# First bias tiles loaded from GpSimd's queue, and the second pair's q, k loaded earlier and cast by VectorE

## The chip, the cores and the metric

The kernel runs on one core of a Trainium2 chip. The metric is the time of one execution on the device in microseconds (us), as the median of several runs. A core has five engines with instruction queues of their own: TensorE (matmuls and transposes; PE in the profile, PEld its weight loads), VectorE (DVE), ScalarE (ACT), GpSimd (POOL) and SyncE (SP), which here only issues transfers. All transfers run on the core's 16 DMA engines. A queue works in order: an instruction that waits holds up all that stands behind it on its engine.

## What is computed

The reference is attention with a learned bias on relative positions, followed by a feed-forward layer with the mish function:

```python
# q, k, v: (4, 8, 576, 64); w_in: (512, 2048); w_out: (2048, 512); all float32
scores = scale * np.matmul(q, k.transpose(0, 1, 3, 2))
rel = (pos[:, None] - pos[None, :]).astype(np.float32)
psi_rel = np.log1p(np.abs(rel))
psi_i = np.log1p(np.maximum(pos[:, None].astype(np.float32), 1.0))
x = (psi_rel / psi_i)[..., None]
h = np.maximum(x @ w1 + b1, 0.0)
bias = h @ w2                                   # (576, 576, 8)
scores = scores + bias.transpose(2, 0, 1)[None, :, :, :]
scores = scores - np.max(scores, axis=-1, keepdims=True)
attn = np.exp(scores)
attn = attn / (np.sum(attn, axis=-1, keepdims=True) + 1e-09)
attn_out = np.matmul(attn, v)
...
h = x @ w_in                                    # x: the 2304 tokens of attn_out
g = h * np.tanh(np.log1p(np.exp(np.minimum(h, 20.0))))
out = g @ w_out
```

## The kernel before

The kernel has three phases: the bias for all heads, the attention, and the feed-forward layer. The change touches the first phase and its seam with the second.

**The bias phase** (loop at line 551, 36 tiles of 16 query rows). For each tile `make_h` (line 510) writes four tiles ht on VectorE or ScalarE, `mirrored` (line 524) multiplies them by w2 on TensorE into PSUM, and `evac` (line 534) copies the result out as bt, on ScalarE nearly always (line 538; once on VectorE, line 540), and has SyncE store it to DRAM, in the buffer bias_d (line 545). Eight buffers bt are in use. The rows of one bias tile of the attention come from 8 such tiles (4 for the tile number 4); the order of the five tiles is ORDER = 0, 1, 4, 2, 3.

**The bias loads.** `load_bias` (line 194) brings one tile of the first head pair back from DRAM, in three pieces of 288, 256 and 32 KB for 128 rows (lines 200 to 202), or in two pieces of 144 KB for tile number 4 (line 205). All are issued by SyncE, at the iterations BIAS_AT = 12, 20, 24, 30 and 37. Each waits for the stores that wrote its rows, and SyncE's other transfers stand behind it.

**q and k.** A pair is one batch and two heads; there are 16. For the matmuls in float32r each pair's q, k (128x1280) are split in a rounded part qkhi and a rest qklo. `load_hi` (line 182) has GpSimd load q, k with a cast to float32r, `load_raw` (line 170) has SyncE load them as they are in rawqk, and `split_qk` (line 188) has VectorE subtract one from the other. Three buffers qkhi and two buffers rawqk are in use. GpSimd's queue holds nothing else in the first phases, so that its loads for the pairs 0, 1 and 2 all start at the beginning, and the next when a buffer comes free. For pair 1, `load_raw` and `load_v` (line 176) stand at iteration 36 of the loop (lines 570 to 572), behind the last store; the last bias tile is loaded at iteration 37, and behind it `load_weights` (line 94) loads two weight tiles of 512 KB.

**The attention** goes in steps, five for each pair, one for each block of query rows in ORDER. A step has `scores` on TensorE (line 224, three products of the split parts), `add_bias` on VectorE, which adds the bias out of the tile and keeps the extreme value of each row (line 238, for 128 rows two halves of 576 columns, each reading its own part of the bias tile), `exps` on ScalarE (line 253), then, two steps later, `transposes` (lines 293 to 320), whose results ScalarE or VectorE copies out of PSUM (line 307 and others), and `pv_duo`, the products with v (lines 335, 339), at whose end VectorE copies the result x (line 342). There are two PSUM buffers s for scores; a step with 128 rows needs both, so its scores wait for the bias addition of the step before. Steps 0, 1 and 2 are spread over the bias phase (SOFT_AT = 18, 27, 35); step 3 and on run in `step` (line 413). `ahead` (line 379) loads what later pairs need, and `split` (line 400) calls `split_qk(i + 1)` at the third step of a pair, for the first pair at step 3. Step 4 (`late`) has its parts in another order than all others: transposes of step 2, products with v, and only then its scores and bias addition. Step 5 is the first of pair 1 and needs qkhi and qklo of pair 1; step 7 splits pair 2, and step 10 needs it.

Of the kernel before, what the change touches and what calls it, by code (L numbers as in the profile page):

```python
# [8 lines left out]
F32R = mybir.dt.float32r  # L9
# [6 lines left out]
B, H, S, D, C = 4, 8, 576, 64, 32  # L16
# [3 lines left out]
P = 128  # L20
SH = S // 2
QW = 1280
# [6 lines left out]
ORDER = [0, 1, 4, 2, 3]  # L29
# [15 lines left out]
def kernel(ctx: ExitStack, tc, qk, v, wb, w2, w_in, w_out, psia, psi4, rinv, eye, out):  # L45
    nc = tc.nc
    pe, dve, act, pool, sp = nc.tensor, nc.vector, nc.scalar, nc.gpsimd, nc.sync
# [115 lines left out]
    hip = rsbuf("hip", 2, side="right")  # L163
# [3 lines left out]
    qk_raw, qk_hi, qk_lo, v_t, bias_t = {}, {}, {}, {}, {}  # L167
    st.tile([P, 32], F32, name="fill", bufs=1)

    def load_raw(i):  # L170
        hp, b = divmod(i, B)
        raw = rawp.tile([P, QW], F32, name="rawqk")
        sp.dma_start(out=raw, in_=qk[b, hp])
        qk_raw[i] = raw

    def load_v(i):
        hp, b = divmod(i, B)
        vt = vp.tile([P, 2, 5, D], F32, name="vt")
        sp.dma_start(out=vt, in_=v[b, hp].rearrange("p (h c d) -> p h c d", h=2, c=5))
        v_t[i] = vt  # L180

    def load_hi(i):
        hp, b = divmod(i, B)
        hi = hip.tile([P, QW], F32R, name="qkhi", bufs=3)
        pool.dma_start(out=hi, in_=qk[b, hp])
        qk_hi[i] = hi

    def split_qk(i):

        lo = hip.tile([P, QW], F32R, name="qklo")  # L190
        dve.tensor_tensor(lo, qk_raw.pop(i), qk_hi[i].bitcast(F32), op=ALU.subtract)
        qk_lo[i] = lo

    def load_bias(hp, c):
        h0, h1 = 2 * hp, 2 * hp + 1
        rows = P if c < 4 else 64
        src = bias_d[c][:, :rows * PITCH].rearrange("h (i j) -> h i j", j=PITCH)[:, :, PAD:PAD + S]
        t = bias_t[hp, c] = biasp.tile([P, 2 * S if c < 4 else 640], F32, name=f"bias{c}")[:, :2 * S if c < 4 else S]
        if c < 4:
            sp.dma_start(out=t[:, 0:S], in_=src[h0])  # L200
            sp.dma_start(out=t[:, S + 64:], in_=src[h1, :, 0:512])
            sp.dma_start(out=t[:, S:S + 64], in_=src[h1, :, 512:S])
        else:
            for r in range(2):
                sp.dma_start(out=t[r * 64:r * 64 + 64], in_=src[h0 + r])

    NPAIR = B * HP
    steps = [(i, c) for i in range(NPAIR) for c in ORDER]
# [46 lines left out]
    def reciprocals(i):  # L255

        r = sums.pop(i)
        dve.tensor_scalar(r, r, 1e-9, None, op0=ALU.add)
        dve.reciprocal(r, r)
        return r  # L260
# [151 lines left out]

    def step(n):
        i, x = divmod(n, 5)
        late = n == 4

        def begin():
            if n < NS:
                scores(n)
                add_bias(n)  # L420

        def end():
            if n < NS:
                exps(n, 0)
                exps(n, 1)
                ahead(n)
            if 0 <= n - 1 < NS and (n - 1) % 5 == 4:
                rc[n - 1] = reciprocals((n - 1) // 5)
            if n < NS:
                split(n)  # L430
            if turned:
                store_reciprocals()


        if not late:
            begin()
        for k in {3: (0, 1)}.get(n, (n - LAG,)):
            if 0 <= k < NS:
                transposes(k)
        if not late:  # L440
            end()

        if late:
            for k in range(5):
                pv_duo(0, 0, k)
        for j, grp, ks in {4: ((i, 0, (0, 1)),), 0: ((i - 1, 0, (2, 3)),), 1: ((i - 1, 0, (4,)),),
                           2: ((i - 1, 1, (0, 1, 2)),), 3: ((i - 1, 1, (3, 4)),)}[x]:
            if 0 <= j < NPAIR and (j, grp) != (0, 0):
                for k in ks:
                    pv_duo(j, grp, k)  # L450
        if late:
            begin()
            end()

# [20 lines left out]
    NB = len(ts)  # L477
    NW = S + 15

    def reach(t):  # L480

        left, right = 16 * t + 15, S - 16 * t
        n = max(left + 1, right)
        return left, right, n + n % 2
# [5 lines left out]
    BIAS_AT = (12, 20, 24, 30, 37)  # L490
# [6 lines left out]
    for idx in range(NB + 2):  # L497
# [4 lines left out]
        if idx + 2 < NB:  # L502
            n = reach(ts[idx + 2])[2]
# [47 lines left out]
    for idx in range(NB + 2):  # L551
        if idx < NB:
            make_h(idx + 2)
            mirrored(idx)
        if 1 <= idx <= NB:
            evac(idx - 1)
        if idx == 1:
            load_raw(0)
            load_v(0)
        if idx == 12:  # L560
            split_qk(0)
        if idx in BIAS_AT:
            load_bias(0, ORDER[BIAS_AT.index(idx)])
        for lag, do in enumerate((scores, add_bias, exps)):
            if idx - lag in SOFT_AT:
                for u in range(2 if lag == 2 else 1):
                    do(SOFT_AT.index(idx - lag), *((u,) if lag == 2 else ()))
        if idx == 33:
            load_hi(1)
        if idx == NB:  # L570
            load_raw(1)
            load_v(1)
        if idx == NB + 1:
            load_weights()
    bias_scope.close()

# [10 lines left out]
    for n in range(len(SOFT_AT), NS):  # L587
        step(n)
# [246 lines left out]
```

## Time and profile before

| | us |
|---|---|
| median of 3 runs | 699.02 |
| lowest and highest | 698.3, 699.84 |
| the profiled execution | 701.45 |
| its span, first to last instruction | 699.5 |

| engine | busy, share of the span |
|---|---|
| TensorE matmuls | 97% |
| VectorE | 74% |
| ScalarE | 66% |
| GpSimd | 2% |

The bias phase fills the first 55 us or so of the span, the attention goes on to about 270 us, and the rest is the feed-forward layer. Times in the profile are counted from the first instruction. Busy shares are means over phases with different limits; what a change in one place is worth is read from that place, from the waits there.

### The profile page before, as it was taken

The numbers are of one execution on the slowest core, as the hardware profiler recorded it, in microseconds if no ns is written. First come the engines' busy times: TensorE is split into PE (matmuls) and PEld (weight loads), VectorE is DVE, ScalarE is ACT, GpSimd is POOL, SyncE is SP. The second block draws the span as 40 slices with busy tenths as digits, with TensorE's granted clock in tenths as the row PEclk, the third lists the DMA queues.
The fourth block names the chain that finished last, engine by engine and source line by source line (L and its number), as shares of the span: only waits on it lengthen the run. The fifth ranks groups of instructions, "written<-read, shape, count | busy, mean of one in ns | idle before, by whom it ended". The sixth has DMA issues, their size and how long they took to land.

```text
span 699.5 us, 14139 instructions
## 1 busy us (share of the span) xinstructions
PE 675.6 (97%) x5456; PEld 515.5 (74%) x5456; DVE 514.3 (74%) x1051; ACT 463.9 (66%) x980; POOL 16.5 (2%) x26
## 2 busy tenths in 40 slices
PE   6987999999999999899999999999999999999997
PEld 3545766666666676567878888889988888888886
DVE  7894788888888886468888888776776567665554
ACT  6994899999989999645665556554544455444443
POOL 1000000000000002000000000001000000000000
PEclk9999899999999999999999999999999999999999
DMA  7989658659657762412231221323040000010001
GB/s 257 294 263 303 221 178 290 211 172 314 228 180 250 252 208 76 130 48 61 60 121 60 91 66 55 121 73 109 1 121 31 0 1 0 1 61 0 1 0 61
DMA packets 46435, 86.94 MB, mean 124 GB/s; under 512 B 13200, under 2 KB 22048, under 8 KB 46368
## 3 DMA queue, kind: packets, MB, share of 16 engines
q1 hardware_dynamic: 43488, 75.32, 33.5%
q0 software_dynamic: 2304, 10.49, 4.7%
q8 instruction: 43, 0.70, 0.4%
q10 hardware_dynamic: 576, 0.22, 0.1%
q14 instruction: 24, 0.20, 0.1%
HBM read 64.56 MB, written 21.45 MB: 123 GB/s over the span
## 4 chain that ended last, share of the span: by engine, by line
PE 85%; DVE 7%; ACT 3%; DMA 3%; issue 1%; SPq 0%; DVEq 0%; ACTq 0%
PE y L679 25%; PE h L634 24%; PE s L224 11%; PE o L335 10%; PE tp L293 5%; PE bps L532 5%; PE o L339 2%; PE tp L309 2%; DMA rawqk<-in_qk_dram 1%; DMA xlo<-r_d 1%; DVE e L657 1%; DVE e L641 1%; DVE e L656 1%; ACT bt L538 1%; DVE w L127 1%
## 5 line engine op out<-in xcount | busy, mean ns | idle before, releaser
L238 DVE CUSTOM_DVE_ANT_0 pt<-s,bias 128x576 f32<-128x576 f32 x144 | 103.7, 754 | 44.4 <-PE s L224 44.3
L253 ACT ACTIVATE pt<-pt,m 128x576 f32<-128x576 f32 x144 | 112.5, 792 | 6.5 <-DVE m L238 6.2
L658 ACT CAST ghi<-e 128x512 fp32r<-128x512 f32 x72 | 44.7, 621 | 105.5 <-DVE e L657 98.2
L679 PE MATMUL y<-who,ghi 128*128 128x512 f32 x288 | 112.5, 391 | 2.2 <-ACT ghi L658 1.4
L679 PE MATMUL y<-who,glo 128*128 128x512 f32 x288 | 112.4, 390 | 1.1 <-DVE glo L661 1.0
L679 PE MATMUL y<-wlo,ghi 128*128 128x512 f32 x288 | 112.2, 390 | 0.0
L634 PE MATMUL h<-xhi,whi 128*128 128x512 f32 (+1 forms) x320 | 80.0, 370 | 1.3 <-ACT xhi L609 1.3
L661 DVE TENSOR_TENSOR glo<-e,ghi 128x512 fp32r<-128x512 f32 x72 | 49.7, 691 | 42.0 <-ACT ghi L658 41.3
L307 ACT COPY main<-tp 128x512 f32<-128x512 f32 x126 | 68.1, 597 | 18.4 <-PE tp L293 18.0
L634 PE MATMUL h<-xhi,wli 128*128 128x512 f32 (+1 forms) x320 | 79.6, 371 | 0.0
L634 PE MATMUL h<-xlo,whi 128*128 128x512 f32 (+1 forms) x320 | 79.2, 369 | 0.0
L335 PE MATMUL o<-main,vt 128*64 128x320 f32 (+1 forms) x512 | 75.8, 418 | 1.1 <-DVE x L342 1.1
L639 ACT ACTIVATE e<-h 128x512 f32<-128x512 f32 x72 | 42.6, 592 | 45.7 <-PE h L634 45.7
L640 DVE TENSOR_SCALAR e<-e 128x512 f32<-128x512 f32 x72 | 30.7, 426 | 55.8 <-ACT e L639 55.8
L634 PEld LDWEIGHTS h<-xhi,whi 128*128 128x128 f32 x320 | 57.4, 189 | 13.6 <-ACT xhi L609 2.7
L634 PEld LDWEIGHTS h<-xhi,wli 128*128 128x128 f32 x320 | 57.5, 190 | 10.1
L634 PEld LDWEIGHTS h<-xlo,whi 128*128 128x128 f32 x320 | 57.4, 190 | 10.2
L679 PEld LDWEIGHTS y<-who,ghi 128*128 128x128 f32 x288 | 54.1, 188 | 14.4 <-ACT ghi L658 2.2
L679 PEld LDWEIGHTS y<-who,glo 128*128 128x128 f32 x288 | 54.1, 188 | 13.5 <-DVE glo L661 2.3
L679 PEld LDWEIGHTS y<-wlo,ghi 128*128 128x128 f32 x288 | 54.1, 188 | 10.8
L657 DVE TENSOR_TENSOR e<-e,r 128x512 f32<-128x512 f32 x72 | 49.9, 693 | 7.5
L224 PEld LDWEIGHTS s<-qkhi 64*128 64x128 f32 (+1 forms) x288 | 25.0, 189 | 36.9 <-DVE m L238 16.2
(71 smaller groups left out, 1037.6 us busy)
## 6 DMA issues: line engine op xcount, KB each, us to landing
bias_d<-bt SPq DMA_DIRECT2D x36, 295.5 KB
qkhi<-in_qk_dram POOLq DMA_DIRECT2D x16, 640.0 KB, 6.4
rawqk<-in_qk_dram SPq DMA_DIRECT2D x16, 640.0 KB
w<-in_w_in_dram SPq DMA_DIRECT2D x16, 512.0 KB
w<-in_w_out_dram SPq DMA_DIRECT2D x16, 512.0 KB
vt<-in_v_dram SPq DMA_DIRECT2D x16, 320.0 KB
bias<-bias_d SPq DMA_DIRECT2D x16, 288.0 KB
out_dram<-w SPq DMA_DIRECT2D x17, 256.0 KB
```

What stands on the lines that cost most here:

```text
L224: pe.matmul(live[n][h][:, j, :SH], stat[rows, c * P:(c + 1) * P], mov[rows, k0:k0 + SH], start=(k == 0), stop=(k == 2))
L238: dve.tensor_tensor_reduce(out=halves(pt[:, sl]), in0=s[:, :, :SH], in1=halves(bt[:, sl]), scale=-0.125, scalar=BIG, op0=ALU.add, op1=ALU. ...
L253: act.activation(ps, ps, AF.Exp, bias=m[:, u:u + 1], scale=-1.0, accum_out=sums[i][:, k:k + 1])
L293: pe.transpose(tp[:, k * 64:(k + 1) * 64], pt[rows, c0:c0 + P], ident[rows, rows])
L307: (dve.tensor_copy if n < 2 and u else act.copy)(blocks[:, :, off + 64 * u:off + 64 * u + 64], tp)
L335: pe.matmul(o[h * 64:h * 64 + 64, :w], vt[:, h, k, :], main[:, h, k, :], start=(k == 0), stop=False, **kw)
L634: pe.matmul(h[:, u * n:(u + 1) * n], w["i", g4, d][:, r * P:(r + 1) * P], x[:, d, :n], start=(k == 0), stop=(k == 11))
L639: act.activation(e, h, AF.Exp)
L657: dve.tensor_tensor(e, e, r, op=ALU.mult)
L658: act.copy(ghi, e)
L661: dve.tensor_tensor(glo, e, ghi.bitcast(F32), op=ALU.subtract)
L679: pe.matmul(ys[blk][t], g[:, c0:c0 + P], w, start=((blk, f) in first and k == 0), stop=((blk, f) in last and k == 2))
```

## The change

`load_bias` gets a parameter with the queues of its pieces. In the bias phase the tiles 0, 1, 4 and 2 are issued wholly by GpSimd, and the last, tile 3, by SyncE but for its 256 KB piece, which GpSimd issues. (The calls from `ahead` for the later head pairs stay on SyncE.) `load_hi(1)` at iteration 33 is gone: `split_qk` for pair 1 makes qkhi on VectorE as a copy of rawqk with the cast to float32r, and then subtracts as before. `load_raw(1)` moves from iteration 36 to 26. `load_v(1)` moves from iteration 36 to 37, behind the last bias load, and `load_weights` follows it. Step 4 loses its order of its own: its scores and bias addition come first, then the transposes of step 2, the exponentials, and the products with v last.

```diff
     def split_qk(i):
 
+        if i == 1:
+            qk_hi[i] = hip.tile([P, QW], F32R, name="qkhi", bufs=3)
+            dve.tensor_copy(qk_hi[i], qk_raw[i])
         lo = hip.tile([P, QW], F32R, name="qklo")
...
-    def load_bias(hp, c):
+    def load_bias(hp, c, queues=(sp, sp, sp)):
...
         if c < 4:
-            sp.dma_start(out=t[:, 0:S], in_=src[h0])
-            sp.dma_start(out=t[:, S + 64:], in_=src[h1, :, 0:512])
-            sp.dma_start(out=t[:, S:S + 64], in_=src[h1, :, 512:S])
+            queues[0].dma_start(out=t[:, 0:S], in_=src[h0])
+            queues[1].dma_start(out=t[:, S + 64:], in_=src[h1, :, 0:512])
+            queues[2].dma_start(out=t[:, S:S + 64], in_=src[h1, :, 512:S])
         else:
             for r in range(2):
-                sp.dma_start(out=t[r * 64:r * 64 + 64], in_=src[h0 + r])
+                queues[r].dma_start(out=t[r * 64:r * 64 + 64], in_=src[h0 + r])
...
     def step(n):
         i, x = divmod(n, 5)
-        late = n == 4
...
-        if not late:
-            begin()
+        begin()
         for k in {3: (0, 1)}.get(n, (n - LAG,)):
             if 0 <= k < NS:
                 transposes(k)
-        if not late:
-            end()
-
-        if late:
+        end()
+
+        if n == 4:
             for k in range(5):
                 pv_duo(0, 0, k)
...
-        if late:
-            begin()
-            end()
...
         if idx in BIAS_AT:
-            load_bias(0, ORDER[BIAS_AT.index(idx)])
+            load_bias(0, ORDER[BIAS_AT.index(idx)], (sp, pool, sp) if idx > NB else (pool, pool, pool))
...
-        if idx == 33:
-            load_hi(1)
-        if idx == NB:
+        if idx == 26:
             load_raw(1)
+        if idx == NB + 1:
             load_v(1)
-        if idx == NB + 1:
             load_weights()
```

## Rows read from the trace of the kernel before

**Rows 1.** The page: span, TensorE's busy time, its granted clock in 40 slices.

```profile
span 699.5 us, 14139 instructions
PE 675.6 (97%) x5456; PEld 515.5 (74%) x5456; DVE 514.3 (74%) x1051; ACT 463.9 (66%) x980; POOL 16.5 (2%) x26
...
PEclk9999899999999999999999999999999999999999
```

**Rows 2.** Chain of waits from 54 us on: start, us, what.

```profile
57.26 7.68 DMA rawqk<-in_qk_dram
...
68.26 1.68 PE s L224 x11
...
83.91 1.00 PE s L224 x12
...
98.31 0.99 PE s L224 x12
```

**Rows 3.** Timeline of VectorE, 58 to 68: start, us, engine, line, operation [idle before].

```profile
58.50 1.49 DVE L307 COPY main<-tp 128x512 f32<-128x512 f32 x2
65.03 1.49 DVE L191 TENSOR_TENSOR qklo<-rawqk,qkhi 128x1280 fp32r<-128x1280 f32 x1 [5.04 <-DMA rawqk<-in_qk_dram]
...
66.78 0.75 DVE L238 CUSTOM_DVE_ANT_0 pt<-s,bias 128x576 f32<-128x576 f32 x1
...
67.45 0.75 DVE L238 CUSTOM_DVE_ANT_0 pt<-s,bias 128x576 f32<-128x576 f32 x1
```

**Rows 4.** Timeline of TensorE, 63 to 69: scores of steps 4 and 5.

```profile
63.72 0.43 PE L224 MATMUL s<-qkhi,qklo 64*128 64x288 f32 x4
67.59 0.40 PE L224 MATMUL s<-qkhi 64*128 64x288 f32 x1 [3.44 <-DVE m L238]
```

**Rows 5.** Stretches: us, busy of each engine, then PEclk, DMA share, GB/s.

```profile
40.00:56.00 16.00, 14.67 (x291) 8.00 (x283) 13.07 (x34) 13.03 (x22) 0.00 (x0) 1.00 0.87 268
48.00:50.00 2.00, 1.30 (x28) 0.67 (x32) 2.00 (x7) 1.91 (x5) 0.00 (x0) 1.00 0.71 244
54.00:68.00 14.00, 9.30 (x115) 6.52 (x107) 6.65 (x14) 5.91 (x16) 0.53 (x1) 1.00 0.96 297
62.00:74.00 12.00, 8.28 (x82) 6.77 (x79) 5.83 (x15) 4.76 (x15) 0.53 (x1) 0.76 1.01 348
68.00:74.00 6.00, 5.74 (x57) 5.28 (x58) 2.86 (x11) 3.98 (x12) 0.00 (x0) 0.52 1.04 380
```

**Rows 6.** Timeline of SyncE's queue, 56 to 63: its issues.

```profile
56.44 0.77 SPq L545 DMA_DIRECT2D bias_d<-bt  x1
...
61.25 0.33 SPq L200 DMA_DIRECT2D bias<-bias_d  x1
61.63 0.43 SPq L201 DMA_DIRECT2D bias<-bias_d  x1
```

**Rows 7.** Timeline of ScalarE, 54 to 58: the last evacuation.

```profile
54.45 0.75 ACT L538 ACTIVATE bt<-bps,rinv_t 128x591 f32<-128x591 f32 x1 [1.64 <-PE bps L532]
```

**Rows 8.** Chain of waits, 0 to 5 us.

```profile
1.20 3.08 DMA psi_t<-in_psi_dram
```

**Rows 9.** GpSimd's loads: the first three, and all 16 by line 185.

```profile
1.25 1.78 POOL L185 DMA_DIRECT2D qkhi<-in_qk_dram  x3 [0.80 <-POOLq L822]
...
L185 POOL DMA_DIRECT2D qkhi<-in_qk_dram x16: 530/530/722, 1.2 to 241.0; - x16
...
DMA to landing us min/median/max: 4.3/6.4/8.0
```

**Rows 10.** VectorE's groups by shape, 0 to 90: busy, mean ns, idle before.

```profile
L521 DVE TENSOR_SCALAR ht<-at,bb 128x576 f32<-128x576 f32 x6 | 2.7, 510 | 0.0
L521 DVE TENSOR_SCALAR ht<-at,bb 128x304 f32<-128x304 f32 x5 | 1.6, 372 | 0.0
L307 DVE COPY main<-tp 128x512 f32<-128x512 f32 x2 | 1.4, 690 | 0.1
```

**Rows 11.** Waits of VectorE, 0 to 57: us, times, longest.

```profile
DVE pt L238 <- PE s L224: 4.2, 3, 2.0
```

**Rows 12.** Timeline of VectorE, 76 to 80: step 7's split and step 8's bias addition.

```profile
76.39 1.49 DVE L191 TENSOR_TENSOR qklo<-rawqk,qkhi 128x1280 fp32r<-128x1280 f32 x1
...
79.37 0.76 DVE L238 CUSTOM_DVE_ANT_0 pt<-s,bias 128x576 f32<-128x576 f32 x1 [1.15 <-PE s L224]
```

## The prediction

> **What bounds the kernel now.** I read the page first. TensorE is busy for 97% of the span, so a change that does not touch TensorE's waiting can give nothing; and the granted clock of TensorE leaves full speed once, near a tenth of the span [rows 1]. The change lies in that tenth, so I read the chain of waits there. It runs through one transfer: 7.68 us for the raw q, k of the second pair, issued at 57.26, and from there to the scores of step 5 at 68.26 [rows 2]. VectorE's timeline shows the stall itself: after its last copies, which end at 59.99, it sits idle for 5.04 us until rawqk lands, then works through qklo (1.49 us), the x copy and the two halves of step 4's bias addition, which begin at 66.78 and 67.45 [rows 3]. TensorE has nothing in between: its scores of step 4 end at 64.15, and but for one matmul at 67.59 the scores of step 5 wait for VectorE [rows 4]. The table of stretches adds the second half of the price: the clock is 1.00 (2.4 GHz) from 54 to 68 and then 0.52 on average from 68 to 74, nearly all at the lower level of 1.2 GHz, directly after that idle time [rows 5]. What the low clock costs is read from the chain: step 5 to step 10 takes 83.91 - 68.26 = 15.65 us, the next five steps take 98.31 - 83.91 = 14.40 us [rows 2]. So it costs 1.25 us. Behind step 10 the kernel is TensorE bound, and a gain up to there should pass to the end.
>
> Why rawqk lands so late is seen in SyncE's timeline and the DMA share. SyncE issues its last bias store at 56.44, then rawqk and vt, and only at 61.25, released by the landed stores, the first piece of the last bias tile [rows 6]. The DMA engines are 96% busy from 54 to 68 [rows 5]: what stands there is a queue of bytes.
>
> **The change part by part.**
>
> *Raw q, k of pair 1 at iteration 26.* Its 640 KB enter the queue near 43 us and are needed at 60.0, so VectorE's 5.04 us of waiting go. The bytes now stand ahead of the stores of iterations 26 to 35. At the 297 GB/s of the busy stretch [rows 5] they take 2.2 us. Against this, the DMA engines were free for 0.13 x 16 = 2.1 us between 40 and 56, most densely from 48 to 50, where the share is 0.71 [rows 5] and SyncE had bias loads to issue behind stores. I take the two as equal; the bounds are 2 us either way.
>
> *Bias loads on GpSimd.* 11 loads leave SyncE's queue ahead of the last tile, and one of the three pieces of that tile. SyncE no longer holds evacuated tiles back: the last ScalarE evacuation ends at 55.20 [rows 7], and its store, issued at 56.44 before, can go at about 55.25. From 56.44 to the release at 61.25 it took 4.81 us with everything around it [rows 6]; the smallest transfer shown, psi_t with 72 KB on a nearly idle queue, took 3.08 us [rows 8]. I keep 4.8 us, because the engines stay full: release at 60.1, and between 58.3 and 62.1 by these bounds and the 2 us above. GpSimd's queue holds only loads in this phase, 0.53 us of issue each [rows 9]; behind its waits for stores stand only the qkhi loads of pairs 2 and 3.
>
> *The last tile.* Now nothing stands between the stores and its load; vt and weights follow it. Before, its halves were issued from 61.25 and 61.63 on [rows 6] and used at 66.78 and 67.45 [rows 3], so they took at most 5.5 and 5.8 us, behind 960 KB of rawqk and vt; how long they had been there isn't seen, since no wait is shown. On GpSimd's queue 640 KB take 4.3 us at best and 6.4 us in the median from issue to landing [rows 9]. The piece on GpSimd has 256 KB, but the engines are shared with its neighbours, so I take 4.3 us: the second half there at 60.15 + 4.3 = 64.45, with 3.1 to 5.8 us as bounds.
>
> *The cast on VectorE.* A copy of 128x1280 is added. The nearest rows are ht, which also reads one source in SBUF: 372 ns for 304 columns and 510 ns for 576, so 0.507 ns a column and 510 + 704 x 0.507 = 867 ns; by the copy out of PSUM, 690 ns for 512 columns, it would be 1.73 us [rows 10]. I take the first. It starts at 59.99, then comes qklo: done at 62.3, at most 63.2. Both are hidden by the wait for the tile that lands at 64.45; if the tile were there at 60, they would be the path themselves.
>
> *Step 4 in the ordinary order.* Scores first, then transposes, then the value products. TensorE does the same blocks in another order, so it is through at 64.15 at the earliest, as before [rows 4]; the x copy goes behind the bias addition, and nobody near waits for it. I count it at nothing. The same goes for the two qkhi loads that leave the first 3 us: the start waits for psi_t [rows 8], not for them.
>
> *Sum at step 5.* Before, the second half of the bias addition began at 67.45 and the scores went on at 68.26, 0.81 us later. Now that is 64.45 + 0.05 + 0.81 = 65.3. The gain is 2.95 us, and at most 68.26 - 64.15 = 4.1 us, where TensorE itself comes last. TensorE's pause shrinks from 4.1 us to 1.2 us. From 48 to 50 it paused for 0.70 of 2.00 us without a fall of the clock [rows 5], so I count the 1.25 us as gained too.
>
> *What is late next.* qkhi of pairs 2 and 3 now load behind the bias tiles, at about 61; pair 2's was among the first three loads, from 1.25 us on, before [rows 9]. From 61.2 on, the bias tile (576 KB), vt (320), two weights (1024), two qkhi (1280) and raw q, k of pair 2 (640) have to pass: 3840 KB, which at the 348 GB/s of 62 to 74 [rows 5] take 11.3 us, until 72.5, and about 73 with the landing. VectorE wants them for the next qklo at 76.39 - 4.2 = 72.2 [rows 12]. That is a wait of 0.8 us, or 2.6 us at 300 GB/s; VectorE has 1.15 us of idle time ahead of step 8's bias addition [rows 12] to make up for it. I put 0.5 us on the path, between 0 and 2.
>
> Sum: 2.95 + 1.25 - 0.5 = **3.7 us**. The profiled execution took 701.45 us, its span of 699.5 and 1.95 around it, and becomes 697.75. The median of the runs is 2.43 us below it, at 699.02; the same gain there gives **695.3 us**.
>
> **The rivals.**
>
> 1. *The last tile stays as late.* The raw bytes push the stores back (release at 62.1) and the tile needs 5.5 us: second half at 67.6 against 67.45 before. Then TensorE's pause and the low clock stay, and what is left is between nothing and 2 us; I write 1.0 us: 698.0. For it speaks the DMA share of 0.96; against it the 2.1 us of free share and the store that goes 1.2 us earlier.
>
> 2. *The clock falls all the same.* If a pause of 1.2 us or somewhat more is enough, the 1.25 us stay lost: 2.95 - 0.5 = 2.45 us, 696.6.
>
> 3. *Slower: GpSimd and VectorE hold each other up in the bias phase.* VectorE makes ht there nearly without a break, and 11 loads of 0.53 us come into it, 5.8 us of issue. If VectorE stood still for all of it and none fell into its idle time (4.2 us before the bias additions up to 57 [rows 11]), the phase would end 5.8 us later: 695.3 + 5.8 = 701.1. The sign turns where 3.7 us are lost, that is, from two thirds of the issue time on. Against it: each tile's loads start once its stores have landed, some 8 to 10 us before its use, so that a delay can be made up in the idle time ahead of the next bias addition. No row of before has a GpSimd issue beside an ht instruction, so its cost is open from 0 to 5.8 us. The Trainium skill (SBUF — State Buffer, section "SBUF: two separate sides") speaks against the change at this point: a DMA issued from GpSimd has its descriptors written by GpSimd's cores, and these are locked out while VectorE runs a copy-like fp32 instruction in its two-port mode; it advises SyncE's or ScalarE's queue. By that rule the GpSimd piece of the last tile would also wait for the cast, until about 60.9 in place of 60.15, and the sum would be 0.7 us smaller; no row of before shows it.
>
> 4. *The change doesn't do what it says*, because some other transfer or wait takes the place of rawqk at once: 699.0.
>
> **How the numbers follow.** About 0.2% (1.4 us) is what a measurement of this kernel can tell from no change. Forecast 695.3, own range 693.6 to 697.2: 0.60; its fast end is a gain of 4.1 + 1.25 = 5.35 us. Rival 1: 0.19, two thirds of it within 0.2%. Rival 2: 0.10, faster. Rival 3: 0.07, slower. Rival 4: 0.04, same. So faster 0.60 + 0.10 + 0.06 = 0.76, same 0.13 + 0.04 = 0.17, slower 0.07. The range leaves out rival 3 and the ends of the others: 693.5 to 698.9.
>
> **What would show it.** Right: no wait of qklo for rawqk near 60; the last store issued at 55 to 55.5 and the last tile's load near 60; step 5's scores near 65.3; a granted clock of 1.00 throughout 66 to 76; step 5 to step 10 in 14.4 to 15 us. Wrong: ht instructions longer than 372 to 510 ns, or gaps between them at GpSimd's issues (rival 3); step 4's second bias addition after 66.5 (rival 1); a clock near 0.5 after a short pause (rival 2); the second qklo waiting for rawqk or qkhi by more than 2 us.

## The result, and the profile after

The changed kernel takes 703.75 us (702.46 to 705.15) against 699.02 us in the same measurement: a ratio of 1.0067, 95% interval 1.0047 to 1.0087. It is slower by 4.7 us, where 3.7 us of gain were forecast. Its profiled execution took 702.8 us.

The page shows what is unchanged (TensorE's busy time) and one thing that is not: GpSimd was busy for 16.5 us [rows 1] and now is for 33.3 us, with 11 instructions more.

```profile
span 700.9 us, 14165 instructions
PE 675.6 (96%) x5456; PEld 514.6 (73%) x5456; DVE 515.2 (74%) x1052; ACT 464.8 (66%) x980; POOL 33.3 (5%) x37
...
PEclk9999999999999999999999999999999999999999
```

Eleven more issues at 0.53 us [rows 9] would be 5.8 us, not 16.8. The timeline of GpSimd after the change shows which are longer (start, us, engine, line, operation, in brackets the idle time before and what ended it):

```profile
24.34 6.23 POOL L203 DMA_DIRECT2D bias<-bias_d  x1 [22.38 <-DMA bias_d<-bt]
30.56 0.55 POOL L204 DMA_DIRECT2D bias<-bias_d  x1
...
41.61 6.22 POOL L208 DMA_DIRECT2D bias<-bias_d  x2 [7.08 <-DMA bias_d<-bt]
58.02 0.57 POOL L203 DMA_DIRECT2D bias<-bias_d  x1 [10.18 <-DMA bias_d<-bt]
...
65.93 0.54 POOL L204 DMA_DIRECT2D bias<-bias_d  x1 [6.27 <-DMA bias_d<-bt]
```

The first issue of the first tile took 6.23 us, and of the two of the small tile the first took 5.71 us. Beside them VectorE's timeline, 22 to 49 us:

```profile
22.96 7.49 DVE L518 TENSOR_SCALAR ht<-at,bb 128x336 f32<-128x336 f32 x20
35.59 0.76 DVE L241 CUSTOM_DVE_ANT_0 pt<-s,bias 128x576 f32<-128x576 f32 x1 [5.14 <-DMA bias<-bias_d]
...
36.95 0.76 DVE L241 CUSTOM_DVE_ANT_0 pt<-s,bias 128x576 f32<-128x576 f32 x1 [0.59 <-DMA bias<-bias_d]
...
37.64 9.58 DVE L518 TENSOR_SCALAR ht<-at,bb 128x304 f32<-128x304 f32 x30
48.31 0.76 DVE L241 CUSTOM_DVE_ANT_0 pt<-s,bias 128x576 f32<-128x576 f32 x1 [1.10 <-PE s L227]
```

The two streams of ht end at 22.96 + 7.49 = 30.45 and at 37.64 + 9.58 = 47.22. GpSimd's two long issues end at 24.34 + 6.23 = 30.57 and at 41.61 + 5.71 = 47.32, about 0.1 us later. These two issues, which began in the middle of VectorE's stream, were held until the stream had ended. The first tile then came late, and VectorE itself stood still for 5.14 + 0.59 us. Before, the same additions, and those of step 3, came at these times:

```profile
32.40 0.76 DVE L238 CUSTOM_DVE_ANT_0 pt<-s,bias 128x576 f32<-128x576 f32 x1 [1.98 <-PE s L224]
...
33.08 0.75 DVE L238 CUSTOM_DVE_ANT_0 pt<-s,bias 128x576 f32<-128x576 f32 x1
...
44.44 0.76 DVE L238 CUSTOM_DVE_ANT_0 pt<-s,bias 128x576 f32<-128x576 f32 x1 [1.10 <-PE s L224]
...
57.14 0.76 DVE L238 CUSTOM_DVE_ANT_0 pt<-s,bias 128x576 f32<-128x576 f32 x1 [1.02 <-PE s L224]
...
57.83 0.75 DVE L238 CUSTOM_DVE_ANT_0 pt<-s,bias 128x576 f32<-128x576 f32 x1
```

The second half of step 0 is 36.95 - 33.08 = 3.87 us late, and so is step 1 (48.31 against 44.44). A second loss follows at step 3. VectorE's timeline after the change, 57 to 72 us, to be held against [rows 3]:

```profile
63.49 0.76 DVE L241 CUSTOM_DVE_ANT_0 pt<-s,bias 128x576 f32<-128x576 f32 x1 [3.48 <-DMA bias<-bias_d]
...
64.81 0.76 DVE L241 CUSTOM_DVE_ANT_0 pt<-s,bias 128x576 f32<-128x576 f32 x1 [0.55 <-DMA bias<-bias_d]
...
66.69 0.96 DVE L192 CAST qkhi<-rawqk 128x1280 fp32r<-128x1280 f32 x1
67.69 1.49 DVE L194 TENSOR_TENSOR qklo<-rawqk,qkhi 128x1280 fp32r<-128x1280 f32 x1
69.10 0.75 DVE L241 CUSTOM_DVE_ANT_0 pt<-s,bias 128x576 f32<-128x576 f32 x1
...
69.77 0.75 DVE L241 CUSTOM_DVE_ANT_0 pt<-s,bias 128x576 f32<-128x576 f32 x1
```

Step 3's second half began at 57.83 before and begins at 64.81 now: 6.98 us late, 3.87 from above and 3.11 new. The new part is the wait for the fourth tile, which GpSimd could issue only at 58.02, when the stores of its rows had landed (57.23). Its pieces then took 5.4 to 5.9 us from issue to landing; SyncE's of before, issued from 50.69 on, had taken 2.9 to 3.8 us. From there the kernel regains time. Nothing waits for rawqk any more, the cast takes 0.96 us, and step 4's second half is 69.77 - 67.45 = 2.32 us late, step 10's scores (at 85.51 in the chain of waits) 85.51 - 83.91 = 1.60 us [rows 2]. That is about the difference of the two profiled executions, 702.8 - 701.45 = 1.35 us. The table of stretches (busy time of PE, PEld, DVE, ACT, POOL, then PEclk, DMA share, GB/s) shows the price in TensorE's clock:

```profile
36.00:44.00 8.00, 4.91 (x88) 2.56 (x84) 7.41 (x25) 5.02 (x9) 2.39 (x1) 0.79 0.75 245
...
62.00:66.00 4.00, 0.88 (x16) 0.71 (x16) 1.96 (x5) 0.98 (x3) 0.07 (x1) 1.00 0.44 174
66.00:70.00 4.00, 3.77 (x29) 2.93 (x31) 3.97 (x7) 2.81 (x10) 1.53 (x3) 0.57 0.89 221
70.00:74.00 4.00, 3.91 (x48) 2.68 (x44) 2.09 (x6) 2.20 (x6) 0.00 (x0) 1.00 1.00 344
```

The low stretch after 68 [rows 5] is gone, but there are two others: 0.79 from 36 to 44, behind the first wait, and 0.57 from 66 to 70, behind the second. While TensorE waited from 62 to 66, the DMA share was 0.44: the engines had room, but what was left to issue stood on both queues behind a wait for the last stores, until 65.41 on SyncE and 65.93 on GpSimd.

The medians differ by 4.7 us and the profiles by 1.35 us because the profiled execution of before was 2.43 us above its median, and that of after 0.95 us below. In the 25 runs of before that stand beside the first four experiments, 12 executions with a mean clock of 0.995 have spans of 697.1 to 698.5 us and 8 with 0.998 have 694.8 to 696.8; the profiled one has 0.993 and 699.5. All five executions of after have 0.990 to 0.993; of the 76 executions of before beside all experiments, 7 have 0.993 or less. At 0.993 the spans are 697.0 to 699.5 us before and 700.4 to 702.1 after, so the rest of the 4.7 us goes with the lower clock of after. In which stretches the clock fell is on record for the profiled executions alone.

### The profile page after: what moved, and what is told of

Its sections match the earlier page's. It is cut to its first block, busy times and chain, and to the rows that moved or that the text cites. A ratio compares the mean times of both kernels' runs of the same rounds, so it can differ in the third digit from the quotient of the medians.

```text
span 700.9 us, 14165 instructions
## 1 busy us (share of the span) xinstructions
PE 675.6 (96%) x5456; PEld 514.6 (73%) x5456; DVE 515.2 (74%) x1052; ACT 464.8 (66%) x980; POOL 33.3 (5%) x37
## 4 chain that ended last, share of the span: by engine, by line
PE 82%; DVE 6%; ACT 3%; DMA 1%; issue 1%; POOL 0%; DVEq 0%; ACTq 0%
PE y L674 25%; PE h L629 24%; PE s L227 11%; PE o L338 10%; PE tp L296 5%; PE o L342 2%; PE tp L312 2%; PE bps L529 2%; DVE e L652 1%; DVE e L636 1%; DMA bias<-bias_d 1%; DVE e L651 1%; DVE w L127 1%; DVE w L134 1%; ACT pt L256 1%
## 5 line engine op out<-in xcount | busy, mean ns | idle before, releaser
L310 ACT COPY main<-tp 128x512 f32<-128x512 f32 x126 | 68.1, 597 | 17.6 <-PE tp L296 16.5
L529 PE MATMUL bps<-ht,w2t 128*32 128x79 f32 (+41 forms) x864 | 45.2, 355 | 11.2 <-DVE ht L518 5.8
```

The costliest lines, as they stand in the source:

```text
L310: (dve.tensor_copy if n < 2 and u else act.copy)(blocks[:, :, off + 64 * u:off + 64 * u + 64], tp)
L529: pe.matmul(ps[cg * 32:cg * 32 + 32, a:b], w2t, src, start=True, stop=True)
```

## Experiments

**Question A: does VectorE's ht hold GpSimd's issues, and is that the loss?** The theory: GpSimd can't finish a load's issue while VectorE streams ht, which reads one tile in SBUF. The rivals: GpSimd's transfers are slow for another reason, or the loss comes from the raw q, k alone.

*Only the queues of the bias loads* (before, with this part of the change alone):

```diff
-            load_bias(0, ORDER[BIAS_AT.index(idx)])
+            load_bias(0, ORDER[BIAS_AT.index(idx)], (sp, pool, sp) if idx > NB else (pool, pool, pool))
```

> The kernel before with one part of the change alone: the bias loads on GpSimd's queue (three tiles behind the qkhi loads of pairs 0 to 2), rawqk, vt, qkhi and step 4 as before. Theory A: the first GpSimd load is held until VectorE's ht ends near 30.5, step 0's bias addition waits to about 35.6 in place of 32.4, and the bias phase ends 3.9 us later: 702 to 704 us. Rival C: no loss here, 698 to 700 us.

Measured: 707.28 us (703.3 to 709.95), ratio 1.0109, 1.0075 to 1.0144. The timeline of GpSimd:

```profile
23.86 6.62 POOL L200 DMA_DIRECT2D bias<-bias_d  x1 [21.91 <-DMA bias_d<-bt]
...
41.42 6.54 POOL L205 DMA_DIRECT2D bias<-bias_d  x2 [7.78 <-DMA bias_d<-bt]
...
54.27 2.76 POOL L200 DMA_DIRECT2D bias<-bias_d  x1 [6.31 <-issue]
```

The same holds, without any of the other edits; the third, 2.76 us, is on the fourth tile, and ends 0.1 us behind a stream of ht too. This part alone costs 8.2 us in the median of four executions, more than expected; the profiled one is the fastest of them, 703.3 us. Not all of it need be the holds. The expectation has the tiles behind the qkhi loads of pairs 0 to 2, but in this run only pair 0's goes ahead of them. That of pair 1 stands at iteration 33, is issued at 58.09 behind four tiles, and loads beside the last stores and rawqk, which lands at 68.83 (64.94 before).

*The first tile back on SyncE* (the changed kernel otherwise):

```diff
-... (sp, pool, sp) if idx > NB else (pool, pool, pool))
+... (sp, pool, sp) if idx > NB else (sp, sp, sp) if idx == BIAS_AT[0] else (pool, pool, pool))
```

> The changed kernel with only the first bias tile back on SyncE. Theory A: the 5.14 us wait of step 0 goes, the hold of tile 4's GpSimd load (5.71 us in the changed kernel) stays but that tile has slack; step 1's scores end near 44.4. The 3.5 us wait at step 3 for the tile loaded by GpSimd stays by theory B. So 698.5 to 701 us. Rival C: 702 to 704 us.

Measured: 698.45 us (696.91 to 700.41), ratio 0.9991, 0.997 to 1.0012. Three transfers on another queue give back 5.3 us, with the raw q, k, the cast and the order of step 4 as in the changed kernel. GpSimd's timeline:

```profile
34.53 0.55 POOL L203 DMA_DIRECT2D bias<-bias_d  x1 [32.57 <-DMA bias_d<-bt]
...
42.01 2.17 POOL L208 DMA_DIRECT2D bias<-bias_d  x2 [5.79 <-DMA bias_d<-bt]
```

The small tile was still held, for 1.66 us, until the stream of ht had ended; this time it was in time. But the three issues from 34.53 on went through in 0.55 to 0.60 us beside ht instructions of 0.37 us, and so did the same three pieces in the three later runs with the first tile alone on SyncE (0.54 to 0.60 us). So not every issue beside ht is held; what decides between the two is open. The 15 that were held, in seven runs, all end 0.10 to 0.12 us behind the end of the stream.

*ht written with two inputs* (the changed kernel, a tile of zeros as the second source, so that the result is the same):

```diff
+    zt = bc.tile([P, S], F32, name="zt")
+    dve.memset(zt, 0.0)
-                dve.tensor_scalar(ht[:, :n], at[:, :n], bb[:, k:k + 1], 0.0, op0=ALU.add, op1=ALU.max)
+                dve.scalar_tensor_tensor(ht[:, :n], at[:, :n], bb[:, k:k + 1], zt[:, :n], op0=ALU.add, op1=ALU.max)
```

> The changed kernel with VectorE's ht made by an instruction with two tensor inputs in SBUF (a tile of zeros as the second) in place of one with a single input. VectorE stays as busy or busier, since this form is slower (near 0.7 to 0.8 us for 576 columns in place of 0.51), so the time is not the question. Theory A1 (it is the single-input form of ht that holds GpSimd's issue): the first bias load takes about 0.55 us of issue in place of 6.23 us, in the midst of ht. Theory A2 (any VectorE work without a break holds it): the issue again lasts until VectorE pauses, 5 us or more.

Measured: 716.35 us in one run; ht is slower in this form (536 ns for 304 columns, where it was 373). What counts is GpSimd's timeline, and VectorE's beside it:

```profile
27.33 0.55 POOL L203 DMA_DIRECT2D bias<-bias_d  x1 [25.38 <-DMA bias_d<-bt]
...
49.77 1.04 POOL L208 DMA_DIRECT2D bias<-bias_d  x2 [7.03 <-DMA bias_d<-bt]
```

```profile
21.71 10.49 DVE L520 SCALAR_TENSOR_TENSOR ht<-at,bb,zt 128x448 f32<-128x448 f32 x19
```

The first issue starts at 27.33, in the middle of a stream that lasts to 32.20, and takes 0.55 us. VectorE's stream has no break here either, the transfers are the same, only the form of the instruction differs (and with it the length of the phase), and the hold is gone: all 11 issues beside ht took 0.52 to 0.57 us. This tells theory A1 from A2, and from the rival that GpSimd's loads are slow by themselves.

*Raw q, k out of the way, first tile still on GpSimd* (the changed kernel with `load_raw(0)` and `load_raw(1)` ahead of the loop):

```diff
+    load_raw(0)
+    load_raw(1)
...
-        if idx == 26:
-            load_raw(1)
```

> The changed kernel with rawqk of pairs 0 and 1 issued before the first tile, nothing else. Theory A's loss stays (the first tile's load held until ht pauses, step 0 late by 3 to 4 us), theory B's goes (step 3 waits under 1 us for its tile): 698 to 701 us against 703.8 for the changed kernel. If theory A's hold is not a loss of its own: 695 to 697 us.

Measured: 703.97 us (702.23 to 704.98), ratio 1.0066, 1.0041 to 1.0091. The first issue was held for 7.55 us (22.98 to 30.53), and the small tile's two took 7.31 us. The time is that of the changed kernel, not the 698 to 701 us expected. With the holds in place, moving the raw q, k changes nothing in the time, but not because it has no effect: the holds were longer here. Step 1 is at 51.59, 3.28 us later than in the changed kernel, while step 3's second half follows step 1 in 14.75 us in place of 16.50, and still waits 1.33 + 0.98 us for its tile. So this run doesn't price the raw loads by themselves.

**Question B: what do the raw q, k at iteration 26 cost and give?** The prediction set 2.2 us of bytes against 2.1 us of free DMA share. The rival: the stores behind them land later, and whoever waits for the stores waits too.

*All bias loads on SyncE* (the changed kernel otherwise):

```diff
-            load_bias(0, ORDER[BIAS_AT.index(idx)], (sp, pool, sp) if idx > NB else (pool, pool, pool))
+            load_bias(0, ORDER[BIAS_AT.index(idx)])
```

> The changed kernel with all bias loads issued by SyncE again; the early rawqk, the cast on VectorE and step 4's ordinary order stay. Theory A (GpSimd's issue of the first bias tile is held while VectorE makes ht without a break: 6.23 us for one instruction in the changed kernel, and step 0's bias addition waits 5.14 us for the tile): that wait is gone, step 1's scores end near 44.4 as before the change instead of 48.3. Theory B (the 640 KB of rawqk ahead of the stores make the tiles behind them late, 3.5 us of waiting at step 3): that wait stays in part, since SyncE now holds the later stores behind the load. Taken together 695 to 697 us. Rival C (the moved rawqk and the cast are the loss, the queue of the loads is not): 702 to 704 us.

Measured: 703.34 us (700.81 to 705.26), ratio 1.0052, 1.003 to 1.0073. The holds are gone, step 1 comes at 44.38, and yet the kernel is slow. SyncE's queue:

```profile
44.27 0.58 SPq L173 DMA_DIRECT2D rawqk<-in_qk_dram  x1
44.94 4.68 SPq L542 DMA_DIRECT2D bias_d<-bt  x4
53.83 0.33 SPq L203 DMA_DIRECT2D bias<-bias_d  x1
...
55.22 4.82 SPq L542 DMA_DIRECT2D bias_d<-bt  x6
63.29 0.33 SPq L203 DMA_DIRECT2D bias<-bias_d  x1
```

and before the change:

```profile
50.69 0.33 SPq L200 DMA_DIRECT2D bias<-bias_d  x1
...
52.31 4.90 SPq L545 DMA_DIRECT2D bias_d<-bt  x6
```

From issue to the increment of the last of its 16 DMA engines, the four stores behind rawqk took 6.2 to 7.6 us; the stores of before, from 42.85 to 48.67, took 3.4 to 5.6 us. SyncE stands at the fourth tile's load until the two of them with its rows have landed (53.27), and issues it at 53.83 in place of 50.69. The last six stores stand behind that load, and so the last tile's load comes at 63.29 in place of 61.25 [rows 6].

The loss is not where the expectation has it. Step 3 doesn't wait for its tile, whose pieces take 2.6 to 2.9 us from issue to landing: its second half is at 57.77, 13.39 us behind step 1's first half, as before the change. Step 4 waits 2.54 us for the last tile, and its second half is at 70.19 in place of 67.45. The time lies in the range of rival C, but rival C isn't the cause: the run with the first tile alone on SyncE has the same raw q, k and cast and took 698.45 us in the same measurement. Of these two, the run that leaves tiles 1, 4, 2 and a piece of the last one on GpSimd is 4.9 us faster.

*Only the raw q, k at iteration 26* (before, with this part alone):

```diff
-        if idx == NB:
+        if idx == 26:
             load_raw(1)
+        if idx == NB:
             load_v(1)
```

> The kernel before with one part alone: rawqk of pair 1 loaded at iteration 26 in place of 36; qkhi by GpSimd, bias loads on SyncE, old order of step 4. Theory A: the bias phase ends as before, the 5.04 us wait for rawqk is gone, the last tile comes 1 to 3 us earlier: 695.5 to 698 us. Theory B (the rawqk bytes push the last stores and the last tile back): 698 to 700 us.

Measured: 700.54 us (699.62 to 702.04), ratio 1.0011, 0.9996 to 1.0025. VectorE's timeline:

```profile
62.04 1.48 DVE L191 TENSOR_TENSOR qklo<-rawqk,qkhi 128x1280 fp32r<-128x1280 f32 x1
...
68.57 0.76 DVE L238 CUSTOM_DVE_ANT_0 pt<-s,bias 128x576 f32<-128x576 f32 x1 [0.49 <-PE s L224]
...
69.25 0.75 DVE L238 CUSTOM_DVE_ANT_0 pt<-s,bias 128x576 f32<-128x576 f32 x1
```

qklo runs at 62.04 without a wait, 3 us earlier than before, and step 4's second half is still 1.8 us later. The row has its first half wait for TensorE's scores, which end at 68.5: TensorE had waited until 60.11 for ScalarE's copies, which the profile has waiting 3.04 us for a bias store, and then its clock fell.

```profile
60.00:70.00 10.00, 8.65 (x60) 5.36 (x60) 4.15 (x8) 3.98 (x13) 0.53 (x1) 0.66 0.88 281
```

The last tile is late as well: loaded from 63.28 on, it lands at 67.71 to 68.39, right ahead of its use. In the trace of before it had landed at 66.42 to 67.24, only 0.2 us ahead of its use at 67.45 [rows 3]. The chain went through rawqk, but the tile stood right behind it.

*Both raw loads at the start, all bias loads on SyncE* (the diffs of the last run of A and the first of B together):

> The changed kernel with all bias loads on SyncE and with rawqk of pairs 0 and 1 issued before the first tile, in the stretch from 6 to 11 us in which the DMA engines have little to do, in place of iterations 1 and 26. Theory B (rawqk in front of the stores of iterations 26 to 29 made SyncE wait for them until 53.4 to 53.8 us in place of 50.7, and so the last tile 2 to 3 us late): SyncE's load of the fourth tile is at 50.5 to 51 again, the last store lands by 60.5, the last tile's load goes at 60 to 61, step 4's second bias addition starts by 65.5, and the time is 695 to 697.5 us against 703.3 with rawqk at iteration 26. Rival D (the cast on VectorE or the new order of step 4 is the loss): 701 us and more.

Measured: 699.64 us (697.72 to 702.0), ratio 1.0016, 0.9998 to 1.0033. Against the run with rawqk at iteration 26 this is 3.7 us less, though not the 695 to 697.5 us expected. SyncE's queue:

```profile
51.25 0.33 SPq L203 DMA_DIRECT2D bias<-bias_d  x1
...
60.70 0.33 SPq L203 DMA_DIRECT2D bias<-bias_d  x1
```

The fourth tile's load is back near its old place, the last one's is at 60.70. But step 4 still waits:

```profile
64.27 0.76 DVE L241 CUSTOM_DVE_ANT_0 pt<-s,bias 128x576 f32<-128x576 f32 x1 [1.82 <-DMA bias<-bias_d]
...
68.35 0.76 DVE L241 CUSTOM_DVE_ANT_0 pt<-s,bias 128x576 f32<-128x576 f32 x1 [3.31 <-DMA bias<-bias_d]
```

**Question C: why is the last tile late even when it is issued early?** In that run GpSimd loads qkhi of pair 3 at 61.09, half a microsecond from the tile. The theory: its 640 KB share the DMA engines with the tile.

*The first tile on SyncE, both raw loads at the start* (first tile as in the second run of A, raw loads as in its last):

> The changed kernel with the first bias tile back on SyncE and rawqk of pairs 0 and 1 issued before the first tile: neither of the two losses. Theories A and B together: no wait for a tile at steps 0 and 3 beyond 0.5 us, the last tile's load at 58 to 60, 694 to 697 us, at or below the other one with rawqk first. Rival D: 698 us and more.

Measured: 697.38 us (696.13 to 700.02), ratio 0.9976, 0.9957 to 0.9995: faster than both kernels, and just above the range expected. Step 3 still waits 0.85 us for its tile, and step 4's second half is still at 67.76, with two qkhi loads issued at 62.44.

*qkhi of pair 3 held back* (all bias loads on SyncE, raw loads at the start, and a small copy on GpSimd that reads the result of step 4 ahead of the load):

```diff
+        if n == 4:
+            held.append(m)
...
+            if i == 1:
+                pool.tensor_copy(st.tile([P, 2], F32, name="hold", bufs=1), held.pop())
             load_hi(i + 2)
```

> The changed kernel with all bias loads back on SyncE and both rawqk loads at the start (as in the run e6, 699.64 us), and in addition GpSimd's load of qkhi for pair 3 held behind a small copy that reads step 4's result, so that it no longer lies beside the last bias tile. Theory C (the last tile was late in e6 because GpSimd's qkhi load of 640 KB was issued within half a microsecond of it and shared the DMA engines): the tile's pieces land by about 64.5, the second half of step 4's bias addition starts at 64 to 65 instead of 68.35, TensorE's clock stays at full speed from 70 to 74, and the time is 695 to 697.5 us. Rival (the tile is late by itself, since vt and the weights stand behind it and the stores in front): second half still at 67 to 68.5, 699 to 700 us.

Measured: 698.74 us (695.13 to 700.42), ratio 0.9992, 0.9977 to 1.0008.

```profile
63.86 0.76 DVE L241 CUSTOM_DVE_ANT_0 pt<-s,bias 128x576 f32<-128x576 f32 x1 [0.74 <-DMA bias<-bias_d]
...
66.55 0.76 DVE L241 CUSTOM_DVE_ANT_0 pt<-s,bias 128x576 f32<-128x576 f32 x1 [1.92 <-DMA bias<-bias_d]
```

The second half comes 1.8 us earlier, at 66.55 in place of 68.35, not at 64 to 65, and the clock did not stay at full speed from 70 to 74. By this trace theory C is right for half of the delay. The other half stays: of the 16 DMA engines, 15 had delivered the tile's second and third piece by 64.45 and 64.61, the last one at 66.23 and 66.39. Why one engine is 1.8 us behind isn't settled. A load of 16 KB on the queue that the profile calls "instruction" begins at 64.23, and the first piece, landed by then, came evenly (63.70 and 63.73); with raw q, k alone such a load begins at 65.64, and there too the last engine is 1.8 us behind (65.94 and 67.71). That this load is the cause is not shown. The median moved by 0.9 us only, inside the interval, so the gain isn't shown in the time.

*No qkhi load beside the last tile, loads as in the fastest run* (first tile on SyncE, `load_hi(2)` and the raw loads at the start, pair 3 held as above):

> As the run e7 (first bias tile on SyncE, the other bias loads as in the change, both rawqk loads at the start; 697.38 us), with qkhi of pair 2 loaded at the start and qkhi of pair 3 held behind step 4's bias addition, so that no qkhi load lies beside the last bias tile. Theory C: the last tile's piece on GpSimd lands by 64.5 instead of 67.64, step 4's second half starts by 65, and the time is 694 to 696 us. Rival (the piece is late for another reason): second half still at 67 to 68, 697 to 698 us. If the larger load at the start puts off the first tiles of the bias phase, the first bias additions come later than 33 us and the time is above 697.5.

Measured: 697.91 us (695.47 to 700.08), ratio 0.9977, 0.9961 to 0.9992.

```profile
62.89 0.76 DVE L241 CUSTOM_DVE_ANT_0 pt<-s,bias 128x576 f32<-128x576 f32 x1 [0.29 <-DMA bias<-bias_d]
...
65.51 0.76 DVE L241 CUSTOM_DVE_ANT_0 pt<-s,bias 128x576 f32<-128x576 f32 x1 [1.85 <-issue]
```

Step 4's second half is 2.25 us earlier than where the qkhi loads lay beside the tile, and the profiled execution is 695.47 us. Its median is no better, and the expected 694 to 696 us are missed. Of its ten executions three have a mean clock of 1.000 and spans of 694.4 to 694.6, six have 0.995 and spans of 695.7 to 698.3. The profiled one, with 0.996, has the shortest span, 693.7, although its clock was low in this very stretch (0.80 and 0.77 below). So what a fall of the clock here costs the whole isn't settled.

*Step 4 in its old order* (the last run, with step 4's scores and bias addition at its end again):

> The run e10 (697.91 us) with the order of step 4 as before the change (transposes of step 2 and the value products first, the step's scores and bias addition last). Theory of the prediction (the order costs and gives nothing: TensorE does the same blocks, and the step after it waits for the last bias tile either way): second half of step 4's bias addition at 65.5 to 66.5 as in e10, step 10 within 0.7 us of e10's 81.1, time 697 to 699 us. Rival (with the tile no longer the last thing, scores done late put VectorE's bias addition behind TensorE's products): the first half starts after 64.5 instead of 62.89, step 10 is 1 to 2 us later, time 699 to 700 us. Other rival (the products fill TensorE's wait near 58 to 60 and keep its clock at full speed): 696 to 697 us.

Measured: 697.54 us (696.63 to 699.23), ratio 0.9981, 0.9966 to 0.9995: no difference from the new order in the median. Two stretches of the run with the new order, and of this one:

```profile
58.00:62.00 4.00, 2.96 (x38) 2.54 (x39) 3.59 (x6) 2.38 (x7) 0.61 (x1) 0.80 0.35 111
62.00:66.00 4.00, 3.85 (x25) 2.00 (x23) 1.86 (x4) 1.82 (x6) 0.00 (x0) 0.77 0.90 272
```

```profile
58.00:62.00 4.00, 2.63 (x35) 1.71 (x31) 3.23 (x8) 2.44 (x7) 0.99 (x1) 1.00 0.52 174
62.00:66.00 4.00, 3.31 (x33) 2.11 (x32) 2.41 (x3) 1.53 (x6) 0.00 (x0) 1.00 0.97 296
```

The old order kept the clock at 1.00 in this execution, but step 10's bias addition came at 82.08, 1.0 us later than with the new order (81.08): scores late, clock kept, against scores early, clock lost. The first half of step 4's addition is at 65.35 in place of 62.89, as the rival has it, but the second, at 66.50, and the time are as the theory has them.

## Why the prediction was wrong

**Bias loads on GpSimd: the step that failed.** The sum gave them a gain and no cost, and rival 3, with 7 in 100, had the price from the wrong side. It let VectorE stand still for GpSimd's 0.53 us each, 5.8 us in all. What happened is the reverse. ht keeps its length (515 and 373 ns, against 510 and 372 [rows 10]), and GpSimd stands still, not for one ht instruction but to the end of the stream: 6.23 us and 5.71 us. The loss is paid by the tile, and through it by the step. That "a delay can be made up in the idle time" was half right: of 5.7 us of delay in the first issue, 3.87 us reached step 0. And the "8 to 10 us before its use" of the same sentence is too much for the fourth tile, loaded at 50.69 and used from 57.14 on. On GpSimd its pieces took 5.1 to 6.2 us from issue to landing (five runs with a hold of at most 1.2 us there), on SyncE 2.6 to 4.5 us (five traces). GpSimd's go out while SyncE issues stores beside them; whether the stores or the queue make the difference, no run tells. Taking three transfers away from GpSimd was worth 5.3 us, the new queues alone cost 8.2 us. The gain that the sum gave to the others was there: with the first tile alone on SyncE, the kernel was 4.9 us faster than with all tiles there. The sign hung on this step. What the prediction named as the mark of it, longer ht instructions or gaps between them, was a wrong place to look; the mark is a longer issue on GpSimd.

The Trainium skill (SBUF — State Buffer, section "SBUF: two separate sides") has this trap, and the prediction cited it, but worked it out for the cast alone (0.7 us) and not for ht: GpSimd can't write descriptors while VectorE is in a two-port mode. Under "A bandwidth-pool intuition that's wrong (but worth ruling out)" on the same page, the Trainium skill has the wait last until VectorE's end and about 115 ns. The traces agree on the 115 ns, 0.10 to 0.12 us, but behind the end of a whole stream of 18 to 30 back-to-back instructions. Under "Who interferes with whom" the Trainium skill infers from the ports why tensor_tensor, with two inputs in SBUF, doesn't hold up descriptors. The run with ht made by another operation with two inputs in SBUF agrees, 0.55 us in place of 6.23. I gave the rule a small chance because no row of before showed it. No row of before could have shown it, since GpSimd issued nothing beside ht there.

**Raw q, k at iteration 26: mis-sized.** VectorE's wait of 5.04 us for rawqk did go, as said. "I take the two as equal" was the error. Free share is no reserve when the queue that would use it stands waiting for a landing. The stores behind the 640 KB landed 2 to 3 us later, the fourth tile's load waited for them, and the last tile's load came 2.04 us later with SyncE alone (63.29 against 61.25). In the changed kernel the last store of the fourth tile's rows took 7.7 us from issue (49.50) to landing (57.23), and the 3.11 us at step 3 follow from that wait and from the long loads behind it. How much of the 3.11 us is the raw bytes alone is read from the time between step 1's first half and step 3's second. It is 13.4 us in all five traces with the fourth tile on SyncE, with rawqk at iteration 26 or elsewhere; 14.2 to 14.8 us in the five with that tile on GpSimd and rawqk elsewhere; and with both 60.03 - 44.65 = 15.38 us (first tile on SyncE) and 16.50 us (the changed kernel). So at step 3 the raw bytes alone cost nothing, GpSimd's queue 0.8 to 1.4 us, and the two together 2.0 to 3.1 us. Moving the raw loads to the start gave 3.7 us back with all loads on SyncE, where the last tile paid for them, and 1.1 us with the first tile alone there (697.38 against 698.45). The bound of 2 us was too small at the larger of these, and I put it at 0.

**The last store at 55.25 and the release at 60.1.** The last store went at 59.11 and SyncE's last-tile load at 65.41. With the 3.87 us by which the bias phase was late taken off, that is 55.24 and 61.54: the store was right to a hundredth, the release 1.4 us later than forecast and inside its bounds, since the last two stores took 6.0 and 6.15 us from issue to landing. In the run with the first tile on SyncE the load comes at 61.11, 1 us behind the forecast and 0.14 us ahead of before.

**The last tile: 4.3 us, and rival 1.** In the changed kernel the term was right: 4.05 us from the release at 65.41 to the last landing at 69.46, and the bias addition didn't wait for it. Rival 1 (the tile stays late) describes the runs without the hold. Raw q, k alone: no gain, since the tile had landed only 0.2 us ahead of its use already in before. In the run of 699.64 us the tile's load came at 60.70, and its last piece took until 68.19. The neighbour that the prediction moved there itself ("stand only the qkhi loads of pairs 2 and 3") cost 1.8 us of that, by the traces.

**The cast: right.** 0.96 us in this trace and 0.81 or 0.82 in those of the experiments, against 0.87 forecast; in no trace does the chain of waits pass through it.

**Step 4's order: right in the time.** Counted at nothing; 697.54 against 697.91 us. In the traces it moves step 10 by 1.0 us and the clock the other way.

**The clock: misread and mis-sized.** The prediction has it leave full speed once. But the page's digit 9 stands for 90% or more, and the trace of before has a second low stretch, from 290.1 to 293.5 us; after the change it is there from 291.5 to 294.9. The stretch after 68 did go, but two others came. And the profiled execution of before had a lower clock than most: executions of before with a mean clock of 0.998 are some 2 us shorter than those at 0.995, and the profiled one was at 0.993. Whether the median execution lost the 1.25 us after 68 at all isn't on record.

**Late raw of pair 2: 0.5 us on the path.** qklo of pair 2 waited 1.38 us for rawqk, against 0.8 forecast, inside its bounds; the chain of waits doesn't pass through it.

## What to carry to other kernels

A transfer issued from GpSimd is not free of VectorE: where VectorE streams one-input instructions in SBUF, put the loads that the next step waits for on a queue that isn't GpSimd's. Those with time to spare may stay there: the runs that left the other tiles on GpSimd took no longer than those with all on SyncE (698.45 against 703.34, 697.38 against 699.64, 697.91 against 698.74 us). Ahead of moving bytes into "free" DMA time, look for who waits for the landing of what is issued behind them. And before taking a wait away, look at how far behind the next transfer had landed: here 640 KB could come 3 us earlier and gain nothing, since the next tile had landed only 0.2 us ahead of its use.

## What the runs showed of the hardware that was not expected

- A GpSimd load that begins beside VectorE's stream of ht can be held to the end of the stream: 5.71 to 7.55 us for the first two held tiles of the changed kernel and of the one with the raw loads at the start. In four runs three issues each beside ht were not held (0.54 to 0.60 us). The difference isn't explained. Beside ht with two inputs in SBUF, none of 11 was held.
- With 640 KB ahead of them, stores took 6.2 to 7.6 us from issue to landing (all loads on SyncE), in place of 3.4 to 5.6 us before.
- The fourth tile's pieces took 5.1 to 6.2 us from issue to landing when GpSimd issued them, and 2.6 to 4.5 us when SyncE did.
- One of the 16 DMA engines can deliver its part of a transfer 1.8 us behind the other 15 (64.45 and 66.23 us). The transfer counts as landed with the last.
